# A block-sparse attention and expert kernel on one core: 24 expert tiles in straight code and a jump table for the rest, instead of 31 tiles in straight code

## The chip, the cores and the metric

The kernel runs on one core of one Trainium2 chip. The metric is the device time of one execution in microseconds; lower is better. The time of the kernel before is the median of three executions without a profile. The trace is of one further execution, taken by the hardware profiler.

The engines are named as the profile names them: PE is TensorE (PEld its weight loads), DVE is VectorE, ACT is ScalarE, POOL is GpSimd and SP is SyncE. A trailing q (PEldq, POOLq) marks records of an engine's instruction stream: branches, register loads, semaphore steps.

## The reference

Two parts follow one another. The first is attention over 4 x 8 heads of 768 tokens with a block mask; its result is laid out as x, 3072 tokens of 512 numbers. The second sends each token to one of eight experts:

```python
logits = x @ w_gate                      # (3072, 512) @ (512, 8)
expert_idx = np.argmax(logits, axis=1)
gate_w = probs[np.arange(N), expert_idx]
for e in range(E):                       # rows lo:hi of x_sorted belong to expert e
    h = np.maximum(x_sorted[lo:hi] @ w1[e], 0.0)   # w1[e]: 512 x 1024
    y_sorted[lo:hi] = h @ w2[e]                    # w2[e]: 1024 x 512
return gate_w[:, None] * y_sorted[inv_perm]
```

The inputs are random with a fixed seed, so how many tokens each expert receives is fixed by the reference.

## The kernel before

**Attention** (to about 430 us of the trace). Rows of x, with the gate weight behind them, are written to a scratch tensor x_d in memory, and the logits stay on the chip. Line 371 loads a flag, bad, into a register of each engine, and line 372 skips a slower version of the attention where the flag is zero, as it is here: `again = nc.values_load(bad[0:1, 0:1], min_val=0, max_val=1)`, `with tc.If(again > 0):`.

**Routing** (430 to 479 us, lines 386 to 499). VectorE works out which expert each token goes to, nt_e, how many tiles of 128 tokens each expert needs, and upto, its running sum over the experts. The tokens of an expert start at a new tile. At most NT + E - 1 = 24 + 7 = 31 = NC tiles can result. xe holds the expert of each tile; tiles behind the last used one get expert 7. g_idx holds the row that each place of a tile gathers (row 0 where there is none), s_idx the row that it is scattered to (out of bounds, and so dropped, where there is none).

**Experts** (479 us to the end, lines 502 to 578). For each of the NC = 31 tiles: gather(i) (line 512) fetches 128 rows of x_d by an indirect DMA issued on GpSimd; fetch(i) (lines 519 and 521) loads the tile's expert number into a register of SP, which then issues the load of that expert's w1, 2 MB; turn_x(i) (lines 526, 528) turns the rows by four transposes on PE and a copy on VectorE to xT; layer1(i) (line 538) is 64 instructions of matmul, whose first half of results goes through a relu on VectorE (line 543) and whose second half through one on ScalarE (line 545) into hT; layer2(i) loads the expert number into a register of PE (line 548) and multiplies hT with that expert's w2, which lies in SBUF (line 551, 16 instructions); VectorE scales the result by the gate weight into zo (line 556) and GpSimd issues the indirect DMA that scatters it to the output (line 557). Buffers: xg four, w1, xT, hT, zo two each.

**Order.** The program order is gather and fetch two tiles ahead, then turn_x and layer 1 one tile ahead, then layer 2 of the tile. A scheduler works out each engine's own order from that, by readiness and priority, within one stretch of straight code; nothing is moved into or out of a conditional block. Engines run their own streams and meet at semaphores.

Of the kernel before, what the change touches and what calls it, by code (L numbers as in the profile page):

```python
# [8 lines left out]
F32 = mybir.dt.float32  # L9
BF16 = mybir.dt.bfloat16  # L10
I32 = mybir.dt.int32
AX = mybir.AxisListType.X
AF = mybir.ActivationFunctionType
ALU = mybir.AluOpType
# [4 lines left out]
def kernel(  # L19
# [11 lines left out]
    nc = tc.nc  # L31
# [9 lines left out]
    E = moe_w_gate.shape[1]  # L41
# [3 lines left out]
    NT = N // P  # L45
    NC = NT + E - 1
# [6 lines left out]
    const = ctx.enter_context(tc.tile_pool(name="const", bufs=1))  # L53
# [332 lines left out]
    g_idx = const.tile([P, NC], I32, name="g_idx")  # L386
    s_idx = const.tile([P, NC], I32, name="s_idx")
    xe = const.tile([1, NC], I32, name="xe")

    rt = ExitStack()  # L390
    sm = rt.enter_context(tc.tile_pool(name="sm", bufs=1))
# [55 lines left out]
    nc.vector.reduce_sum(nt_e[:], og[:], axis=AX)  # L447
    upto = sm.tile([P, E], F32, name="upto")
    nc.vector.tensor_tensor_scan(upto[:], nt_e[:], zero_e[:], 0.0, op0=ALU.add, op1=ALU.add)

    xk = sm.tile([1, NC, E], F32, name="xk")
    nc.vector.tensor_tensor(  # L452
# [55 lines left out]
    st = [{} for _ in range(NC)]  # L508

    def gather(i):  # L510
        xg = st[i]["xg"] = xp.tile([P, XW], F32, name="xg", bufs=4)
        nc.gpsimd.indirect_dma_start(  # L512
            out=xg[:], out_offset=None, in_=x_d[:, :],
            in_offset=bass.IndirectOffsetOnAxis(ap=g_idx[:, i : i + 1], axis=0),
        )

    def fetch(i):

        e = nc.sync.value_load(xe[0:1, i : i + 1], min_val=0, max_val=E - 1)
        w1 = st[i]["w1"] = wp.tile([P, DB, F], F32, name="w1")  # L520
        nc.sync.dma_start(w1[:], w1v[:, bass.ds(e, 1)].rearrange("p e c f -> p (e c) f"))

    def turn_x(i):
        tp = ps_m.tile([P, DB, P], F32, name="tpg", tag="m")
        for c in range(DB):
            nc.tensor.transpose(tp[:, c, :], st[i]["xg"][:, c * P : (c + 1) * P], ident[:])  # L526
        st[i]["xT"] = xp.tile([P, DB, P], F32, name="xgT")
        nc.vector.tensor_copy(st[i]["xT"][:], tp[:])  # L528

    def layer1(i):  # L530

        hT = st[i]["hT"] = xp.tile([P, FB, P], F32, name="hT")
        for g in range(2):
            hp = ps_h.tile([P, FB // 2, P], F32, name="hp")
            for m in range(FB // 2):
                fb = g * (FB // 2) + m
                for c in range(DB):
                    nc.tensor.matmul(  # L538
                        hp[:, m, :], lhsT=st[i]["w1"][:, c, fb * P : (fb + 1) * P], rhs=st[i]["xT"][:, c, :],
                        start=(c == 0), stop=(c == DB - 1),  # L540
                    )
            if g == 0:
                nc.vector.tensor_relu(hT[:, : FB // 2, :], hp[:])  # L543
            else:
                nc.scalar.activation(hT[:, FB // 2 :, :], hp[:], AF.Relu)  # L545

    def layer2(i):
        e = nc.tensor.value_load(xe[0:1, i : i + 1], min_val=0, max_val=E - 1)
        zp = ps_z.tile([P, DM], F32, name="zp")
        for fb in range(FB):  # L550
            nc.tensor.matmul(  # L551
                zp[:], lhsT=st[i]["hT"][:, fb, :], rhs=w2_all[:, fb, bass.ds(e, 1), :].rearrange("p e d -> p (e d)"),
                start=(fb == 0), stop=(fb == FB - 1),
            )
        zo = xp.tile([P, DM], F32, name="zo")
        nc.vector.tensor_scalar(zo[:], zp[:], scalar1=st[i]["xg"][:, DM : DM + 1], scalar2=None, op0=ALU.mult)  # L556
        ins = nc.gpsimd.indirect_dma_start(  # L557
            out=out[:, :], out_offset=bass.IndirectOffsetOnAxis(ap=s_idx[:, i : i + 1], axis=0),
            in_=zo[:], in_offset=None, bounds_check=N - 1, oob_is_err=False,
        )  # L560
        ins = getattr(ins, "ins", ins)
        tc.declare_no_dep(ins, group="rows_out", reason="disjoint rows")
        tc.add_to_no_dep_group("rows_out", ins)
        st[i].clear()

    for i in range(2):
        fetch(i)
        gather(i)
    turn_x(0)
    layer1(0)  # L570
    for i in range(NC):
        if i + 2 < NC:
            gather(i + 2)
            fetch(i + 2)
        if i + 1 < NC:
            turn_x(i + 1)
            layer1(i + 1)
        layer2(i)


# [28 lines left out]
```

## Time and profile before

| | us |
|---|---|
| median of three executions (lowest, highest) | 933.06 (931.87, 934.28) |
| the profiled execution | 937.63 |
| its span, first to last instruction | 935.9 |
| PE busy (share of the span) | 881.2 (94%) |
| PE weight loads busy | 562.5 (60%) |
| VectorE, ScalarE, GpSimd busy | 303.1, 206.4, 78.0 |

The page gives busy time by engine, 40 slices of the span, the DMA queues, the chain of work that ended last and the costliest groups of instructions. A matmul's end in the records is modelled, so PE's busy share says when it had work, not how well it was used.

### The profile page before, as it was taken

The page shows a single profiled execution, that of the slowest core. Times are in us where ns is not written, and L with a number is a line of the kernel's source. Part 1 is how long each engine was busy: PE and PEld are TensorE (multiplying, and loading weights), DVE is VectorE, ACT ScalarE, POOL GpSimd, SP SyncE. Part 2 cuts the span into 40 slices and gives each one's busy share as a digit, 9 for nine tenths or more (in the row PEclk, how much of TensorE's full clock was granted, in tenths as well). Part 3 has the DMA queues.
Part 4 walks back from the last instruction along what each step waited for, and adds up shares of the span by engine and source line. Part 5 has one row for each costly group of instructions (what it writes and reads, how often), then busy time and mean ns, then how long its engine had stood idle before and what let it go on. Part 6 is the DMA issues. An engine that isn't in the chain of part 4 may idle for free.

```text
span 935.9 us, 13135 instructions
## 1 busy us (share of the span) xinstructions
PE 881.2 (94%) x5350; PEld 562.5 (60%) x5350; DVE 303.1 (32%) x590; ACT 206.4 (22%) x292; POOL 78.0 (8%) x103
## 2 busy tenths in 40 slices
PE   4999999999999999994479999999999999999997
PEld 2455555555455555542467767677677676776764
DVE  4545555555545555554311111111111111111110
ACT  1534444444544444441000000000000000000000
POOL 5000000000000000001100111101111011010100
PEclk9999999999999999996569999999999999999999
DMA  9992222212222221000146453545545545455320
GB/s 271 374 310 69 68 69 68 60 46 66 69 63 56 69 65 38 18 19 22 58 176 242 178 191 132 213 164 178 197 147 211 183 151 215 157 192 200 138 93 1
DMA packets 96392, 122.57 MB, mean 131 GB/s; under 512 B 56451, under 2 KB 72835, under 8 KB 96324
## 3 DMA queue, kind: packets, MB, share of 16 engines
q1 hardware_dynamic: 86612, 90.28, 29.9%
q0 software_dynamic: 9184, 31.33, 9.7%
q8 instruction: 46, 0.75, 0.3%
q14 instruction: 22, 0.18, 0.1%
q10 hardware_dynamic: 528, 0.02, 0.0%
HBM read 108.93 MB, written 14.52 MB: 132 GB/s over the span
## 4 chain that ended last, share of the span: by engine, by line
issue 46%; POOL 5%; PE 1%; DVE 1%; POOLq 0%; DVEq 0%
POOL xg L512 3%; POOL out_dram L557 1%; PE tok_ps L492 1%; DVE oh_r L487 0%; POOLq L604 0%; DVE oh_c L479 0%; DVE oh_c L483 0%; DVE sl L467 0%; POOLq L512 0%; POOLq L557 0%; DVE pr__10054 L432 0%; PE cps L437 0%; PE cps L438 0%; POOL lt_strict L409 0%; DVE xk L452 0%
## 5 line engine op out<-in xcount | busy, mean ns | idle before, releaser
L538 PEld LDWEIGHTS hp<-xgT,w 128*128 128x128 f32 x1984 | 228.4, 194 | 20.2 <-DVE xgT L528 11.6
L538 PE MATMUL hp<-xgT,w 128*128 128x128 f32 x1984 | 230.0, 277 | 3.5 <-issue 2.5
L551 PE MATMUL zp<-w_all,hT 128*128 x496 | 222.3, 592 | 0.0
L200 ACT ACTIVATE e<-s 128x768 f32<-128x768 f32 x192 | 155.5, 811 | 95.6 <-PE s L198 92.3
L195 PE MATMUL s<-qT,kT 64*128 64x384 f32 x768 | 168.3, 517 | 0.0
L206 DVE TENSOR_TENSOR esum<-esum,e 128x768 f32<-128x768 f32 x128 | 122.7, 958 | 72.6 <-ACT e L200 65.6
L215 PE MATMUL op<-e,v_sb 128*64 128x384 f32 x768 | 144.8, 499 | 0.0
L551 PEld LDWEIGHTS zp<-w_all,hT 128*128 128x128 f32 x496 | 89.8, 190 | 91.3 <-issue 91.3
L545 ACT ACTIVATE hT<-hp 128x512 f32<-128x512 f32 x31 | 18.5, 597 | 468.3 <-PE hp L538 461.8
L556 DVE TENSOR_SCALAR zo<-zp,xg 128x512 f32<-128x512 f32 x31 | 23.3, 751 | 252.8 <-PE zp L551 252.8
L195 PEld LDWEIGHTS s<-qT,kT 64*128 64x128 f32 x768 | 64.5, 189 | 65.1 <-ACT e L200 37.9
L215 PEld LDWEIGHTS op<-e,v_sb 128*64 128x64 f32 x768 | 46.6, 136 | 80.1 <-issue 79.9
L543 DVE TENSOR_SCALAR hT<-hp 128x512 f32<-128x512 f32 x31 | 21.4, 691 | 137.3 <-issue 117.0
L557 POOL DMA_INDIRECT out_dram<-zo,s_idx x31 | 31.5, 1017 | 398.2 <-DVE zo L556 398.2
L198 PE MATMUL s<-pen,oh 64*128 64x384 bf16 x384 | 63.8, 326 | 0.0
L206 DVE TENSOR_TENSOR esum<-e 128x768 f32<-128x768 f32 x32 | 30.6, 958 | 68.6 <-ACT e L200 68.6
L231 PEld LDWEIGHTS xr<-ones,esum 128*128 128x128 f32 x384 | 45.4, 192 | 1.8 <-DVE esum L206 1.2
L231 PE MATMUL xr<-ones,esum 128*128 128x1 f32 x384 | 45.0, 244 | 0.0
L396 POOL IOTA first_w_i<- 128x8 int32 x1 | 0.1, 134 | 423.7 <-SPq L372 423.7
L198 PEld LDWEIGHTS <-oh 64*128 64x128 bf16 x384 | 19.6, 95 | 25.6 <-issue 1.7
L512 POOL DMA_INDIRECT xg<-x_rows,g_idx x31 | 30.3, 976 | 32.0 <-DVE s_idx L498 22.3
L526 PEld LDWEIGHTS tpg<-ident,xg 128*128 128x128 f32 x124 | 16.4, 151 | 25.7 <-issue 25.0
(112 smaller groups left out, 328.0 us busy)
## 6 DMA issues: line engine op xcount, KB each, us to landing
w<-in_moe_w_dram SPq DMA_DIRECT2D x31, 2048.0 KB, 7.8
w_all<-in_moe_w_dram POOLq DMA_DIRECT2D x8, 2048.0 KB, 31.0
k_sb<-in_k_dram SPq DMA_DIRECT2D x32, 192.0 KB, 3.7
q_sb<-in_q_dram SPq DMA_DIRECT2D x32, 192.0 KB, 3.2
v_sb<-in_v_dram SPq DMA_DIRECT2D x16, 384.0 KB, 3.1
x_rows<-xb SPq DMA_DIRECT2D x16, 384.0 KB, 3.7
xg<-x_rows,g_idx POOLq DMA_INDIRECT x31, 3.4
out_dram<-zo,s_idx POOLq DMA_INDIRECT x31, 2.8
```

Of the source, the lines that this page charges most:

```text
L195: nc.tensor.matmul(s[:, hh, :CW], lhsT=kT[r, c * P : (c + 1) * P], rhs=qT[r, cols], start=True, stop=False)
L198: nc.tensor.matmul(s[:, hh, :CW], lhsT=oh[r, c, :], rhs=pen[r, cols], start=False, stop=True)
L200: nc.scalar.activation(e[:], s[:, :, :CW], AF.Exp, scale=scale)
L206: nc.vector.tensor_add(t[:], es[(n, half, 0)][:] if c == 1 else t[:], e[:])
L215: nc.tensor.matmul(op[hh * D : (hh + 1) * D, :], lhsT=v_sb[:, hh, c, :], rhs=e[:, hh, :], start=(c == 0), stop=(c == NCH - 1),)
L231: nc.tensor.matmul(xr[:, HC * M + 2 * m + hh : HC * M + 2 * m + hh + 1], lhsT=esum[:, hh, m * P : (m + 1) * P], rhs=ones[:], start=True, s ...
L512: nc.gpsimd.indirect_dma_start(out=xg[:], out_offset=None, in_=x_d[:, :], in_offset=bass.IndirectOffsetOnAxis(ap=g_idx[:, i : i + 1], axis=0),
L538: nc.tensor.matmul(hp[:, m, :], lhsT=st[i]["w1"][:, c, fb * P : (fb + 1) * P], rhs=st[i]["xT"][:, c, :], start=(c == 0), stop=(c == DB - 1),)
L543: nc.vector.tensor_relu(hT[:, : FB // 2, :], hp[:])
L551: nc.tensor.matmul(zp[:], lhsT=st[i]["hT"][:, fb, :], rhs=w2_all[:, fb, bass.ds(e, 1), :].rearrange("p e d -> p (e d)"), start=(fb == 0), ...
L556: nc.vector.tensor_scalar(zo[:], zp[:], scalar1=st[i]["xg"][:, DM : DM + 1], scalar2=None, op0=ALU.mult)
L557: ins = nc.gpsimd.indirect_dma_start(out=out[:, :], out_offset=bass.IndirectOffsetOnAxis(ap=s_idx[:, i : i + 1], axis=0), in_=zo[:], in_of ...
```

## The change

Routing stays as it is, but two small operations on VectorE are added: they take the last entry of upto, the number of tiles that carry tokens, subtract NT = 24, and keep the result between 0 and 7 as an integer, more. The expert stage runs tiles 0 to 23 in straight code as before, except that gather, fetch and turn_x of tile 24 are issued there too, and layer 1 of tile 24 is not. Then every engine loads more into a register and jumps into one of eight arms. The arm with k tiles holds straight code for tiles 24 to 24 + k - 1 and ends with a jump to a common end. Within an arm the order is gather and fetch of the next tile, layer 1 of this one, turn_x of the next, layer 2 of this one. The tiles and buffers are the same ones; the line that forgot a tile's buffers after its scatter is gone, because several arms name the same buffers.

```diff
--- before.py
+++ after.py
@@ -386,6 +386,7 @@
     g_idx = const.tile([P, NC], I32, name="g_idx")
     s_idx = const.tile([P, NC], I32, name="s_idx")
     xe = const.tile([1, NC], I32, name="xe")
+    more = const.tile([1, 1], I32, name="more")
 
     rt = ExitStack()
     sm = rt.enter_context(tc.tile_pool(name="sm", bufs=1))
@@ -447,6 +448,12 @@
     nc.vector.reduce_sum(nt_e[:], og[:], axis=AX)
     upto = sm.tile([P, E], F32, name="upto")
     nc.vector.tensor_tensor_scan(upto[:], nt_e[:], zero_e[:], 0.0, op0=ALU.add, op1=ALU.add)
+
+    more_f = sm.tile([1, 1], F32, name="more_f")
+    nc.vector.tensor_scalar(
+        more_f[:], upto[0:1, E - 1 : E], scalar1=float(-NT), scalar2=0.0, op0=ALU.add, op1=ALU.max,
+    )
+    nc.vector.tensor_scalar_min(more[:], more_f[:], float(NC - NT))
 
     xk = sm.tile([1, NC, E], F32, name="xk")
     nc.vector.tensor_tensor(
@@ -561,21 +568,32 @@
         ins = getattr(ins, "ins", ins)
         tc.declare_no_dep(ins, group="rows_out", reason="disjoint rows")
         tc.add_to_no_dep_group("rows_out", ins)
-        st[i].clear()
+
 
     for i in range(2):
         fetch(i)
         gather(i)
     turn_x(0)
     layer1(0)
-    for i in range(NC):
-        if i + 2 < NC:
+    for i in range(NT):
+        if i + 2 <= NT:
             gather(i + 2)
             fetch(i + 2)
-        if i + 1 < NC:
+        if i + 1 <= NT:
             turn_x(i + 1)
+        if i + 1 < NT:
             layer1(i + 1)
         layer2(i)
+
+    for extra in tc.Switch(nc.values_load(more[0:1, 0:1], min_val=0, max_val=NC - NT), NC - NT + 1):
+        for i in range(NT, NT + extra):
+            if i + 1 < NT + extra:
+                gather(i + 1)
+                fetch(i + 1)
+            layer1(i)
+            if i + 1 < NT + extra:
+                turn_x(i + 1)
+            layer2(i)
 
 
 # ---- launch: one core; inputs and outputs as the reference has them ----
```

## Rows read from the trace of the kernel before

**Rows 1.** The page's slices: busy tenths of PE.

```profile
PE   4999999999999999994479999999999999999997
```

**Rows 2.** Table by stage: us, then busy us (instructions) of each engine.

```profile
core 0: us, PE busy (x) PEld busy (x) DVE busy (x) ACT busy (x) POOL busy (x), PEclk, DMA share, GB/s
503.00:821.00 318.00, 318.00 (x1847) 232.50 (x1845) 44.38 (x66) 13.13 (x22) 43.90 (x44) 1.00 0.51 179
821.00:931.00 110.00, 108.99 (x600) 75.73 (x598) 14.29 (x22) 4.18 (x7) 12.98 (x13) 1.00 0.35 125
```

**Rows 3.** Timeline of two middle tiles: start us, duration us, engine, line, operation.

```profile
719.10 0.75 DVE L556 TENSOR_SCALAR zo<-zp,xg 128x512 f32<-128x512 f32 x1 [7.98 <-PE zp L551]
733.56 0.75 DVE L556 TENSOR_SCALAR zo<-zp,xg 128x512 f32<-128x512 f32 x1 [7.61 <-PE zp L551]
```

**Rows 4.** Timeline of the last tiles, same columns.

```profile
909.45 0.75 DVE L556 TENSOR_SCALAR zo<-zp,xg 128x512 f32<-128x512 f32 x1 [8.83 <-PE zp L551]
910.86 7.22 PEld L538 LDWEIGHTS hp<-xgT,w 128*128 128x128 f32 x64 [0.97 <-DVE xgT L528]
914.79 0.69 DVE L543 TENSOR_SCALAR hT<-hp 128x512 f32<-128x512 f32 x1 [3.99 <-issue]
918.11 13.04 PE L551 MATMUL zp<-w_all,hT 128*128 x30
924.32 0.75 DVE L556 TENSOR_SCALAR zo<-zp,xg 128x512 f32<-128x512 f32 x1 [8.84 <-PE zp L551]
931.18 0.75 DVE L556 TENSOR_SCALAR zo<-zp,xg 128x512 f32<-128x512 f32 x1 [6.12 <-PE zp L551]
```

**Rows 5.** DMA after 896 us: queue, packets, MB; then issues and landing.

```profile
q0 software_dynamic: 320, 0.07, 0.8%
out_dram<-zo,s_idx POOLq DMA_INDIRECT x4, 2.1
```

**Rows 6.** Timeline of VectorE in the routing stage.

```profile
445.19 0.17 DVE L457 TENSOR_SCALAR xe_f<-xe_f 1x31 f32<-1x31 f32 x1
```

**Rows 7.** Lines L371 and L372: durations in ns (min/median/max), first and last start.

```profile
L371 PEldq TENSOR_LOAD <-bad x1: 494/494/494, 433.4 to 433.4; - x1
L372 SPq EVENT_SEMAPHORE  x8: 17/17/17, 437.7 to 438.2; - x8
L372 POOLq COMPARE_BRANCH  x1: 45/45/45, 433.9 to 433.9; - x1
L372 PEldq COMPARE_BRANCH  x1: 3967/3967/3967, 434.0 to 434.0; - x1
L372 SPq COMPARE_BRANCH  x1: 50/50/50, 435.2 to 435.2; - x1
```

**Rows 8.** Line L396, GpSimd's first instructions after that branch.

```profile
L396 POOLq EVENT_SEMAPHORE  x7: 42/43/43, 437.8 to 438.4; - x7
```

**Rows 9.** Lines L512 (gathers) and L521 (w1 loads): us from issue to landing.

```profile
DMA to landing us min/median/max: 3.2/3.4/5.3
...
DMA to landing us min/median/max: 7.4/7.8/15.4
```

**Rows 10.** Lines L548 and L604: instruction streams of PE and GpSimd.

```profile
L548 PEldq TENSOR_LOAD <-xe x9: 297/300/307, 800.3 to 917.7; - x9
...
L604 POOLq DRAIN  x3: 51/109/2942, 932.0 to 935.6; - x3
L604 PEldq DRAIN  x2: 13/3964/7915, 923.3 to 935.4; - x2
```

**Rows 11.** Table by stage around PE's idle time, columns as in rows 2.

```profile
431.00:432.00 1.00, 0.00 (x0) 0.00 (x0) 0.93 (x6) 0.14 (x1) 0.00 (x0) 0.50 0.15 45
...
482.00:486.00 4.00, 4.00 (x26) 4.00 (x25) 0.40 (x1) 0.00 (x0) 0.00 (x0) 0.64 0.02 4
```

**Rows 12.** Timeline of the first layer 1.

```profile
478.91 17.38 PE L538 MATMUL hp<-xgT,w 128*128 128x128 f32 x128 [2.49 <-issue]
485.61 0.69 DVE L543 TENSOR_SCALAR hT<-hp 128x512 f32<-128x512 f32 x1 [11.73 <-PE hp L538]
```

## The prediction

> **What bounds the kernel now.** I read the page's time slices first: the TensorE (PE) row is at nine tenths almost throughout, with one dip in the middle [rows 1]. Then the table by stage [rows 2]: from 503 to 821 us PE is busy 318.00 of 318.00 us, from 821 to 931 us 108.99 of 110. These are the expert tiles, and no other engine is busy there for more than a seventh of the time, so a microsecond of PE work taken out of this stage is a microsecond of the kernel. One tile is 64 matmuls of layer 1 (910.86 to 918.11, 7.25 us [rows 4]), 16 of layer 2 and four transposes. In the timeline [rows 3] the zo of successive tiles starts at 719.10 and 733.56, a period of 14.46 us. Near the end [rows 4] the period is 14.87 (909.45, 924.32): layer 1 there waits for the copy of xT (0.97 us of idle weight loads at 910.86). After the last zo at 931.18 the span ends at 935.9, 4.7 us later.
>
> How many of the 31 tiles carry tokens follows from the reference: its router sends 431, 32, 256, 32, 256, 160, 593 and 1312 tokens to the eight experts, which is 4+1+2+1+2+2+5+11 = 28 tiles of 128. The trace agrees: after 896 us the scatters of tiles 27 to 30 (four issues) move 0.07 MB [rows 5]; the 32 rows left over in tile 27 (1312 - 10 x 128), 2 KB each, are 0.066 MB, so tiles 28 to 30 write nothing. The count less 24 is 4: the arm with four tiles runs.
>
> **The change, part by part.** I call E the end of layer 2 of tile 23, the last PE work ahead of the jump.
>
> Removed: three tiles of PE work, at the end of the stage where one costs 14.87: 3 x 14.87 = 44.6 us (43.4 at the earlier period).
>
> Moved: in the arm the order is layer 1 of tile i, transposes of i+1, layer 2 of i. Layer 2 no longer has another tile's layer 1 between it and its own. Its first matmuls read the half of hT that VectorE writes when layer 1 is half done; the half that ScalarE writes after layer 1, in a relu of the size of VectorE's (0.69 us [rows 4]), is needed only eight matmuls later, 8 x 13.04/30 = 3.5 us after layer 2 began [rows 4]. So this order costs nothing, and xT of i+1 has a whole layer 2 for its copy: the 0.41 us per tile (14.87 - 14.46) lost at the end now should not come in the arm's three later tiles, at most -1.2 us. I take -0.6. The w1 of tile 25 waits only for layer 1 of tile 23, some 14 us before E, and lands 7.8 us later [rows 9]: hidden. Later fetches have the same distance. If that cover were gone, 7.8 us a tile would show.
>
> Added on VectorE: two one-element operations in the routing chain, which runs without a gap to the token matmuls. Nearest row: L457, an operation of the same kind on 31 elements, 0.17 us [rows 6]: twice that, +0.35 (0 to 0.4).
>
> Added on every engine: a register load and an indirect jump. The kernel has one such place, the load of `bad` and the skipped block at L371 and L372 [rows 7]. There PE's load took 0.49 us and its branch 3.97. On SP and GpSimd the branch itself is 50 and 45 ns, but the next instruction comes late: SP's from 435.2 to 437.7, GpSimd's from 433.9 to 437.8 [rows 7, 8]. So a jump costs 2.5 to 4.0 us of an engine's instruction stream. [...]
>
> What of that reaches PE's array? PE's instruction stream runs ahead of it: it arrived at the closing DRAIN at 923.3, while the array worked until 918.11 + 13.04 = 931.15 [rows 4, 10]. The lead is 7.8 us. The jump needs 0.49 + 3.97 and some 0.3 for register arithmetic, 4.8 in all; the loads of expert numbers in the arm, 0.30 each [rows 10] and as much again for arithmetic, are another 2.4 if all four come first. 7.2 is less than 7.8: I take 0. The lower end is 0, because the jump does no work; the upper end is the full 4.8 with an idle array, plus the clock. [...] The first half of that layer took 485.61 - 478.91 = 6.70 us to its relu [rows 12] against 914.79 - 910.86 = 3.93 [rows 4], 2.8 us more. Upper end 7.6.
>
> Queued behind the jump elsewhere: ScalarE and SP pass it long before E, their work for tile 23 being done or queued. VectorE passes after zo of 23, about E + 4, and its next work is due with half of layer 1, about E + 3.9: slack in any case, since layer 2 comes later. GpSimd matters: the gather of tile 25 now stands behind the scatter of tile 23 and the jump. The scatter leaves its sequencer 0.8 us after zo begins (931.18 and 932.0 [rows 4, 10]), so at about E + 0.9; load 0.5, jump 3.9, handing over 0.2, landing 3.4 [rows 7 to 9]: the rows are there at E + 8.9. The transposes of tile 25 are due after layer 1 of tile 24, E + 7.25 (910.86 to 918.11 [rows 4]). PE waits 1.6: I take +1.5. Lower end 0 (transposes placed within layer 2, as they are today); upper end a landing of 5.3, as the slowest gather, and a lost clock: 3.5 + 2.8 = 6.3. Gathers of 26 and 27 need no such wait, as each has a full tile.
>
> Added at the end: each engine jumps from the arm to the common end, and semaphores that the shorter arm didn't raise are raised (SP's eight at L372, 437.7 to 438.2). GpSimd is last, after the scatter of tile 27. The jump there is unhidden in part, because the scatter needs 2.1 us to land [rows 5]. Bounds 0 (all behind the landing) to 5 (4.0 of jump and 0.5 of semaphores behind it, and a little); I take the fastest jump, SP's: +2.5.
>
> Sum: -44.6 - 0.6 + 0.35 + 0 + 1.5 + 2.5 = -40.85 us. The profiled execution took 937.63 us with a span of 935.9; the runs without a profile have a median of 933.06. The change is a difference within the span, so 933.06 - 40.85 = 892.2 us.
>
> **The rivals.** First: the jump is not hidden, PE's array is empty when it is taken, or the arm's first instructions arrive late. For it: PE's branch record is itself 3.97 us long, unlike the others', which may mean that PE does more there [rows 7]; that the array was idle at that time, so the rows can't show overlap. Against it: the lead of 7.8. Price 7.6, less the 1.5 for the gather which then has time: 898.3 us. [...]
>
> Second: code comes late inside the arm as well. Four tiles are some 4 x (2 x 64 + 2 x 4 + 2 x 16 + 20) = 750 PE instructions; if two further pieces of code have to be waited for at 4.0 each, it is +8: 900.2 us. Against it: the static tiles run the same number of instructions with PE never idle [rows 2].
>
> Third, on the other side: the idle time at the jump drops the clock to 0.50 and it stays there in the arm. A tile then takes twice 14.46; four are 57.8 more: 892.2 + 57.8 + 3.3 = 953 us. It decides the sign from (40.85 - 3.3)/14.46 = 2.6 tiles at the low clock. Against it: the clock came back within the first layer 1, from 482 to 486 us [rows 11].
>
> Fourth: the change doesn't do what it says; the count comes out as 7 and all 31 tiles run. Then nothing is removed and 0.35 + 1.5 + 2.5 are added: 937.4 us. The bytes of the scatters speak against it [rows 5].
>
> **How the numbers follow.** Forecast 0.66, first rival 0.20, second 0.10, third 0.02, fourth 0.02. Low: all credits and no costs, -44.6 - 1.2 + 0.2 = -45.6, so 887. High: the first rival with the end term at its bound and a late gather as well, 898.3 + 2.5 + 2 = 903, which takes in most of the second. A difference under 0.3% (2.8 us) can't be told from no change here. Faster 0.96: the first three cases; slower 0.03: the last two; same 0.01.
>
> **What would show it.** In the timeline after: PE has no idle time longer than 1 us at the jump, then up to 1.6 before the transposes of tile 25; the zo of the last tile starts near 888 us and 28 of them are there; L538 has 28 x 64 matmuls; the span ends 7 us after the last zo. A granted clock under 1.00 after 503 us, or PE idle for 4 us between tiles 23 and 24, would make the first rival right. 31 zo would make the fourth right. An end term over 5 us or idle time between layer 1 and layer 2 in each tile of the arm would make the sum wrong.

## The result and the profile after

The changed kernel takes 896.71 us (median of four executions, 893.64 to 902.72) against 933.67 for the kernel before on the same chip: a ratio of 0.961, 95% interval 0.956 to 0.967. The gain is 37.0 us; the sum had 40.85. The profiled execution took 896.5 us with a span of 894.8.

The page's first lines and PE's slices (busy tenths), which answer to rows 1:

```profile
span 894.8 us, 12581 instructions
PE   3999999999999999999058999999999999999887
```

The dip of the routing is where it was. New are the two slices at eight tenths just ahead of the last one. The table by stage (columns as in rows 2), cut at the last zo of straight code and the last zo of all:

```profile
500.00:823.30 323.30, 323.30 (x1852) 234.33 (x1852) 44.27 (x66) 13.13 (x22) 43.92 (x44) 1.00 0.51 177
823.30:888.30 65.00, 59.90 (x332) 43.25 (x330) 7.87 (x12) 2.39 (x4) 6.89 (x7) 0.97 0.27 95
888.30:894.80 6.50, 0.00 (x0) 0.00 (x0) 0.71 (x1) 0.00 (x0) 0.98 (x1) 0.86 0.05 15
```

Straight code keeps PE busy throughout, as in rows 2. In the arm PE is idle for 5.1 of 65.0 us and the clock is 0.97. PE's timeline across the jump and through the arm shows where (layer 1 is L545 now, the transposes L533, layer 2 L558; the brackets give the idle time before and what ended it):

```profile
816.22 7.03 PE L558 MATMUL zp<-w_all,hT 128*128 x16
823.09 7.31 PE L545 MATMUL hp<-xgT,w 128*128 128x128 f32 x64
832.66 0.66 PE L533 MATMUL tpg<-ident,xg 128*128 128x128 f32 x4 [2.26 <-DMA xg<-x_rows,g_idx]
833.52 7.13 PE L558 MATMUL zp<-w_all,hT 128*128 x16 [0.20 <-issue]
...
855.67 7.38 PE L545 MATMUL hp<-xgT,w 128*128 128x128 f32 x64 [0.24 <-DMA w<-in_moe_w_dram]
...
863.00 7.03 PE L558 MATMUL zp<-w_all,hT 128*128 x16
872.34 9.01 PE L545 MATMUL hp<-xgT,w 128*128 128x128 f32 x64 [2.31 <-DMA w<-in_moe_w_dram]
```

Layer 1 of tile 24, the first work behind the jump, begins while layer 2 of tile 23 ends: the jump costs the array nothing. Then come three waits: 2.26 us for the gather of tile 25, 0.24 and 2.31 us for the w1 of tiles 26 and 27. The layer 1 behind the last takes 9.01 us instead of 7.31.

The jump itself, by the lines of the load and of the switch (columns as in rows 7):

```profile
L588 PEldq TENSOR_LOAD <-more x1: 307/307/307, 816.0 to 816.0; - x1
L622 PEldq COMPARE_BRANCH  x1: 3634/3634/3634, 816.7 to 816.7; - x1
L588 PEldq BRANCH_PREFETCH_HINT  x1: 55/55/55, 820.4 to 820.4; - x1
...
L622 POOLq COMPARE_BRANCH  x1: 43/43/43, 824.7 to 824.7; - x1
L588 POOLq BRANCH_PREFETCH_HINT  x1: 64/64/64, 827.5 to 827.5; - x1
L622 POOLq INC_SWDGE_SEM  x2: 807/834/860, 827.6 to 829.1; - x2
```

PE's stream loads the count at 816.0, when the array has layer 2 of tile 23 still ahead of it (816.22 to 823.25), and is in the arm at 820.4, when the array still has 2.85 us of that layer to do. GpSimd branches at 824.7 and runs its first instruction in the arm at 827.5. Then it spends 0.8 us on a semaphore step (INC_SWDGE_SEM); the trace before has this instruction only at its start, at 0.2 us, 31 ns long. The trace of the kernel below that runs seven tiles in the arm has none behind its jump: in the traces here the step comes with the arm of four tiles only.

Two lines of GpSimd and one of VectorE: the gather of tile 25, the last zo and the last scatter.

```profile
829.34 0.99 POOL L519 DMA_INDIRECT xg<-x_rows,g_idx  x1 [4.04 <-DMA xg<-x_rows,g_idx]
...
888.26 0.75 DVE L563 TENSOR_SCALAR zo<-zp,xg 128x512 f32<-128x512 f32 x1 [9.68 <-PE zp L558]
...
890.17 0.98 POOL L564 DMA_INDIRECT out_dram<-zo,s_idx  x1 [18.09 <-issue]
```

The w1 loads that the arm issues for tiles 26 and 27, SP's line L528 from 825 us on:

```profile
L528 SPq DMA_DIRECT2D w<-in_moe_w_dram x2: 372/372/373, 847.8 to 863.1; - x2
...
DMA to landing us min/median/max: 7.7/8.4/9.1
```

The load of tile 26 is issued at 847.8, when layer 1 of tile 25 ends (840.48 + 7.31). The sum had it at the end of layer 1 of tile 24, 830.4. From 847.8 to 855.5 it has only a transpose and a layer 2 to hide behind.

### The profile page after: what moved, and what is told of

Its sections match the earlier page's. It is cut to its first block, busy times and chain, and to the rows that moved or that the text cites. A ratio compares the mean times of both kernels' runs of the same rounds, so it can differ in the third digit from the quotient of the medians.

```text
span 894.8 us, 12581 instructions
## 1 busy us (share of the span) xinstructions
PE 835.8 (93%) x5098; PEld 531.3 (59%) x5098; DVE 297.6 (33%) x583; ACT 204.5 (23%) x289; POOL 71.5 (8%) x97
## 4 chain that ended last, share of the span: by engine, by line
issue 38%; DMA 5%; POOL 4%; another core or an unknown queue 2%; PE 1%; DVE 1%; POOLq 0%; DVEq 0%
DMA out_dram<-zo,s_idx 5%; POOL xg L519 3%; PE tok_ps L499 1%; POOL out_dram L564 1%; DVE oh_r L494 0%; DVE oh_c L486 0%; DVE oh_c L490 0%; DVE sl L474 0%; PE cps L438 0%; DVE pr__10055 L433 0%; POOLq L519 0%; POOLq L564 0%; PE cps L439 0%; POOL lt_strict L410 0%
## 5 line engine op out<-in xcount | busy, mean ns | idle before, releaser
L545 PEld LDWEIGHTS hp<-xgT,w 128*128 128x128 f32 x1792 | 208.1, 195 | 17.9 <-issue 13.1
L545 PE MATMUL hp<-xgT,w 128*128 128x128 f32 x1792 | 208.6, 279 | 5.0 <-DMA w<-in_moe_w_dram 2.6
L558 PE MATMUL zp<-w_all,hT 128*128 x448 | 200.3, 593 | 0.2 <-issue 0.2
L558 PEld LDWEIGHTS zp<-w_all,hT 128*128 128x128 f32 x448 | 81.5, 191 | 84.5 <-issue 84.5
L552 ACT ACTIVATE hT<-hp 128x512 f32<-128x512 f32 x28 | 16.7, 597 | 437.1 <-PE hp L545 430.6
L563 DVE TENSOR_SCALAR zo<-zp,xg 128x512 f32<-128x512 f32 x28 | 21.0, 750 | 219.8 <-PE zp L558 219.8
L550 DVE TENSOR_SCALAR hT<-hp 128x512 f32<-128x512 f32 x28 | 19.4, 691 | 125.3 <-issue 88.7
L564 POOL DMA_INDIRECT out_dram<-zo,s_idx x28 | 28.4, 1015 | 363.3 <-DVE zo L563 345.2
L236 PE MATMUL xr<-mix,oT 128*128 128x144 f32 x192 | 31.4, 300 | 0.0
L533 PE MATMUL tpg<-ident,xg 128*128 128x128 f32 x112 | 19.0, 296 | 12.3 <-DMA xg<-x_rows,g_idx 12.3
```

Of the source, the lines that this page charges most:

```text
L236: nc.tensor.matmul(xr[:, m * M : (m + 1) * M], lhsT=oT[:, m * P : (m + 1) * P], rhs=mix[:, pr, :], start=True, stop=True)
L545: nc.tensor.matmul(hp[:, m, :], lhsT=st[i]["w1"][:, c, fb * P : (fb + 1) * P], rhs=st[i]["xT"][:, c, :], start=(c == 0), stop=(c == DB - 1),)
L558: nc.tensor.matmul(zp[:], lhsT=st[i]["hT"][:, fb, :], rhs=w2_all[:, fb, bass.ds(e, 1), :].rearrange("p e d -> p (e d)"), start=(fb == 0), ...
L564: ins = nc.gpsimd.indirect_dma_start(out=out[:, :], out_offset=bass.IndirectOffsetOnAxis(ap=s_idx[:, i : i + 1], axis=0), in_=zo[:], in_of ...
```

## The experiments

Times are medians in us; the ratio is to the kernel before measured beside it, with its 95% interval. Theory A is that the jump is hidden by PE's lead and that the arm loses time to two things: GpSimd's late gather, and a w1 buffer that tile 24 keeps. Its rivals are named with each run.

**28 tiles in straight code.** No jump; what does the arm cost as a whole?

```diff
-    for i in range(NC):
-        if i + 2 < NC:
+    NU = 28
+    for i in range(NU):
+        if i + 2 < NU:
...
-        if i + 1 < NC:
+        if i + 1 < NU:
```

> The kernel before with its loop over tiles cut to 28, in straight code: no count, no jump, and tiles 28 to 30, which carry no token, are left out. It prices the jump and its arms as a whole. Theory A (the arm costs the gather's wait, two waits for w1 with a slow stretch after one of them, and a later end: 2.3 + 4.2 + 1.8 us in the trace after, less about 1 us from a better order): 933.7 - 44.6 = 889.1 us, some 7.6 below the changed kernel's 896.7. Rival B (the 3.9 us by which the measured median lies above the sum are variation between executions, the jump is free): 893 to 895, within 4 us of the changed kernel.

Measured: 892.21, ratio 0.956 (0.952 to 0.959). That lies between the two theories' numbers and its interval overlaps the changed kernel's, so the time alone decides nothing. It lies above A's 889 for two reasons that the record shows. The kernel before took 934.48 beside it and not 933.7, and with 28 tiles in straight code the last scatter is late too. Straight code also ends with the slow period, but A's 889.1 had that in it (14.87 a tile).

```profile
862.43 0.75 DVE L556 TENSOR_SCALAR zo<-zp,xg 128x512 f32<-128x512 f32 x1 [8.83 <-PE zp L551]
877.29 0.75 DVE L556 TENSOR_SCALAR zo<-zp,xg 128x512 f32<-128x512 f32 x1 [8.84 <-PE zp L551]
884.16 0.75 DVE L556 TENSOR_SCALAR zo<-zp,xg 128x512 f32<-128x512 f32 x1 [6.12 <-PE zp L551]
...
886.08 0.98 POOL L557 DMA_INDIRECT out_dram<-zo,s_idx  x1 [6.76 <-issue]
```

The period is 14.86, and the last scatter starts 1.92 us after its zo, where the kernel before has 1.03 (932.21 - 931.18 in its timeline). So 0.9 us of the changed kernel's later end belongs to the 28 tiles and not to the jump. A's sum then becomes 934.48 - 44.6 + 0.9 = 890.8; the four executions lie between 891.34 and 896.70, and the last 1.4 us stay unexplained.

**Gather ahead of the jump.**

```diff
+        gather(i + 2)
         if i + 2 <= NT:
-            gather(i + 2)
             fetch(i + 2)
...
-                gather(i + 1)
+                if i > NT:
+                    gather(i + 1)
```

> The changed kernel with the gather of tile 25 issued ahead of the jump. Theory A: the wait of 2.26 us ahead of the transposes of tile 25 was for that gather alone, which stood behind GpSimd's jump: it is gone, 896.7 - 2.3 = 894.4 us, and the waits for w1 of tiles 26 and 27 remain. Rival B: PE is held there by its own jump, and the gather only ended last: 896 to 897 us, PE idle at the same place with another releaser.

Measured: 891.49, ratio 0.954 (0.951 to 0.957). PE's timeline, the transposes of tile 25 and layer 1 of tile 27:

```profile
830.44 0.60 PE L533 MATMUL tpg<-ident,xg 128*128 128x128 f32 x4
...
868.77 7.38 PE L545 MATMUL hp<-xgT,w 128*128 128x128 f32 x64 [1.50 <-DMA w<-in_moe_w_dram]
```

The wait is gone, so it was the gather's alone. The gain is larger than A's 2.3, because the wait for tile 27's w1 is shorter too (1.50 against 2.31) and the layer 1 behind it runs at full speed (7.38). Why that load landed sooner isn't shown.

**Two w1 buffers in turn.**

```diff
+    w1_two = [wp.tile([P, DB, F], F32, name=f"w1_{j}", bufs=1) for j in range(2)]
...
-        w1 = st[i]["w1"] = wp.tile([P, DB, F], F32, name="w1")
+        w1 = st[i]["w1"] = w1_two[i % 2]
```

> The changed kernel with two w1 buffers named once and used in turn, in place of two buffers taken from a rotating pool. Theory A (tile 24's w1 is taken ahead of the switch and kept until behind it, so the arms have one w1 buffer, and the load of tile 26 waits for layer 1 of tile 25): the load of tile 26 is issued when layer 1 of tile 24 ends, some 17 us earlier, PE's waits of 0.24 and 2.31 us for w1 and the slow layer 1 behind the second (9.01 against 7.31 us) go: 896.7 - 4.2 = 892.5 us. Rival B (the load of tile 26 is late because SP reaches it late, or because its transfer is slowed by gathers): the issue stays at the end of layer 1 of tile 25, 896.7 us.

Measured: 893.54, ratio 0.955 (0.953 to 0.958). SP's loads from 825 us on, and PE's timeline:

```profile
L529 SPq DMA_DIRECT2D w<-in_moe_w_dram x2: 372/372/373, 832.4 to 849.8; - x2
...
834.63 0.66 PE L534 MATMUL tpg<-ident,xg 128*128 128x128 f32 x4 [2.27 <-DMA xg<-x_rows,g_idx]
...
871.32 7.31 PE L546 MATMUL hp<-xgT,w 128*128 128x128 f32 x64
```

The load of tile 26 is issued at 832.4, when layer 1 of tile 24 ends (825.05 + 7.31), and no wait for w1 is left. The wait for the gather stands as before, 2.27. Nothing but the buffers was changed, so the late loads come from the way they were taken. In the changed kernel tile 24's w1 was taken ahead of the switch, and its buffer was not given back inside the arm: the loads of tiles 26 and 27 (847.8 and 863.1) are each issued as the layer 1 one tile ahead ends, as with a single buffer.

**Both.** The two edits above in one kernel.

> The changed kernel with both: the gather of tile 25 ahead of the jump, and two w1 buffers in turn. Theory A: both waits go, 896.7 - 2.3 - 4.2 = 890.2 us, PE without idle time from tile 0 to tile 27 across the jump, and what is left above the 28 tiles in straight code is the end, about 1.8 us. Rival B (something else in the arm is next in line, such as the copy of xT or GpSimd's instructions): 892 to 895 us with a new wait.

Measured: 889.60, ratio 0.951 (0.948 to 0.953): the lowest median of this study, ahead of both given kernels. PE's branch, and its transposes of tile 25 and layer 1 of tile 27, which have no idle time before them:

```profile
L624 PEldq COMPARE_BRANCH  x1: 5425/5425/5425, 818.4 to 818.4; - x1
...
831.97 0.60 PE L534 MATMUL tpg<-ident,xg 128*128 128x128 f32 x4
...
868.17 7.31 PE L546 MATMUL hp<-xgT,w 128*128 128x128 f32 x64
```

PE's branch took 5.42 us here and 3.63 in the changed kernel, for the same jump. It is still hidden, but with 1.1 us to spare: the branch ends at 823.87, layer 2 of tile 23 at 824.99. Over the nine traces with the jump PE's branch took 3.35 to 5.42 us.

**The count comes late.** This takes PE's lead away from the jump: the count is written only behind the zo of tile 23, by an operation that adds zero times an element of that zo to it.

```diff
-    nc.vector.tensor_scalar_min(more[:], more_f[:], float(NC - NT))
+    nc.vector.tensor_scalar_min(more_c[:], more_f[:], float(NC - NT))
...
+    nc.vector.scalar_tensor_tensor(
+        more[:], in0=st[NT - 1]["zo"][0:1, 0:1], scalar=0.0, in1=more_c[:], op0=ALU.mult, op1=ALU.add,
+    )
     for extra in tc.Switch(
```

> The changed kernel with the count made late: one VectorE operation behind zo of tile 23 adds zero times an element of it to the count, and the load ahead of the jump waits for that, so PE's queue is empty when it jumps. Theory A (in the changed kernel PE's jump of 3.63 us is hidden by the 7 us by which its instruction stream runs ahead of its array): now some 1.0 + 0.3 + 0.2 + 3.6 + 0.4 = 5.5 us of PE idle time stand between tiles 23 and 24, and layer 1 of tile 24 runs partly at a granted clock under 1.00, up to 2.8 us more; the 2.3 us of waiting for the gather go, since it now has time: 896.7 + 5.5 + 2.8 - 2.3 = 902.7 us, or 900 if the clock holds. Rival B (the jump costs the array the same wherever the count comes from): at most 1 us more, 897.7 us.

Measured: 901.38, ratio 0.964 (0.962 to 0.966). PE's branch, layer 1 of tile 24 and the stages around it:

```profile
L626 PEldq COMPARE_BRANCH  x1: 3548/3548/3548, 828.0 to 828.0; - x1
...
831.93 8.92 PE L546 MATMUL hp<-xgT,w 128*128 128x128 f32 x64 [5.74 <-issue]
...
830.00:832.00 2.00, 0.07 (x1) 0.10 (x1) 0.00 (x0) 0.00 (x0) 0.00 (x0) 0.50 0.13 29
832.00:834.00 2.00, 2.00 (x10) 2.00 (x11) 0.00 (x0) 0.00 (x0) 0.49 (x1) 0.50 0.20 45
```

The branch takes about as long as in the changed kernel, 3.55 us, but now PE's array stands still for 5.74 us, the granted clock is 0.50 when layer 1 begins, and that layer takes 8.92 instead of 7.31. In this trace tile 24's zo starts 21.96 us after tile 23's (848.19 and 826.23), in the changed kernel 17.39 (840.68 and 823.29). A is right within its two numbers, 900 and 902.7, and the wait for the gather of tile 25 is gone, as it had said. The jump is the same instruction in both kernels; what it cost the array went with the work that PE had queued: nothing in the changed kernel, 5.74 us of idle time here. What the branch spends its 3.55 us on, no run here shows.

**All 31 tiles, seven of them in the arm.** The count is forced to 7.

```diff
-        more_f[:], upto[0:1, E - 1 : E], scalar1=float(-NT), scalar2=0.0, op0=ALU.add, op1=ALU.max,
+        more_f[:], upto[0:1, E - 1 : E], scalar1=float(-NT), scalar2=float(NC - NT), op0=ALU.add, op1=ALU.max,
```

> The changed kernel with the count forced to 7: all 31 tiles run, 24 in straight code and 7 in the arm, the three empty ones as well. It sets the arm against straight code with the same tiles. Theory A (the arm has one w1 buffer, so each tile from 26 on waits for its load): five tiles wait, 0.5 to 4 us each, some 10 in all, + 2.3 for the gather + 0.9 at the end - 2.9 for the order: 934 + 10 = 944 us, slower than the kernel before. Rival B (the waits at tiles 26 and 27 come from something that happens once, at the end or at the jump): 934 + 2.3 + 4.2 + 0.9 - 2.9 = 938 us.

Measured: 938.43, ratio 1.003 (1.001 to 1.005). That is B's number. The trace is A's: five loads, each issued as a layer 1 ends, and a wait at each tile from 26 on (tiles 26, 27 and 30 shown; 28 and 29 wait 0.57 and 0.58 in the same timeline).

```profile
L528 SPq DMA_DIRECT2D w<-in_moe_w_dram x5: 373/373/373, 848.9 to 910.1; - x5
...
856.88 7.38 PE L545 MATMUL hp<-xgT,w 128*128 128x128 f32 x64 [0.42 <-DMA w<-in_moe_w_dram]
...
872.20 7.38 PE L545 MATMUL hp<-xgT,w 128*128 128x128 f32 x64 [0.52 <-DMA w<-in_moe_w_dram]
...
918.35 7.38 PE L545 MATMUL hp<-xgT,w 128*128 128x128 f32 x64 [1.38 <-DMA w<-in_moe_w_dram]
```

So A named the mechanism and priced it too high: 0.4 to 0.6 us a tile. The last tile pays more, 1.38: no transposes of a next tile (0.44 us) stand between layer 2 and its layer 1, and its load took 8.08 us where tile 29's took 7.72.

A also had 2.3 us for the gather of tile 25. Its wait is shorter here:

```profile
833.73 0.66 PE L533 MATMUL tpg<-ident,xg 128*128 128x128 f32 x4 [1.34 <-DMA xg<-x_rows,g_idx]
```

GpSimd has no INC_SWDGE_SEM in this arm, and the gather starts at 830.22, 3.92 us after the scatter ahead of it (826.30); in the changed kernel it is 5.02 (829.34 - 824.32). So about a microsecond of the changed kernel's wait goes with that step.

**All 31 tiles, with both mends.** The count forced to 7 as above, and the two edits of the gather and the buffers.

> The count forced to 7, all 31 tiles, with the gather of tile 25 ahead of the jump and two w1 buffers used in turn. Theory A (then the jump and the arm cost PE nothing, and only the end is later): 934 - 2.9 + 0.9 = 932 us, not to be told from the kernel before. Rival B (arm code has a price of its own for each tile, for instance fetched code or GpSimd's extra instructions): 936 us or more, PE idle time between the tiles of the arm.

Measured: 932.10, ratio 0.996 (0.995 to 0.998): a little faster than 31 tiles in straight code. Two successive zo in the arm, as most there follow one another:

```profile
897.18 0.75 DVE L564 TENSOR_SCALAR zo<-zp,xg 128x512 f32<-128x512 f32 x1 [6.18 <-PE zp L559]
911.63 0.75 DVE L564 TENSOR_SCALAR zo<-zp,xg 128x512 f32<-128x512 f32 x1 [6.18 <-PE zp L559]
```

14.45 us, where the kernel before has 14.87 at its end [rows 4]. B, a price of arm code for each tile, falls. One interval in the arm is longer, 14.97 (867.76 to 882.73). The gather of tile 28, which started late (last section), landed only at 874.71, when its transposes were due. PE's stream waited there, loaded the expert number of tile 27 only behind them (874.76), and layer 2 began 0.4 us late.

**63 DMAs on GpSimd instead of 64.** The kernel with both mends; the w2 load of the last expert goes to SP.

```diff
-        nc.gpsimd.dma_start(w2_all[:, :, e, :], moe_w2[e].rearrange("(a p) d -> p a d", p=P))
+        eng = nc.sync if e == E - 1 else nc.gpsimd
+        eng.dma_start(w2_all[:, :, e, :], moe_w2[e].rearrange("(a p) d -> p a d", p=P))
```

> The kernel with both mends (gather of tile 25 ahead of the jump, two w1 buffers in turn), and the w2 load of the last expert issued on SP instead of GpSimd, so that GpSimd issues 63 DMAs instead of 64. Theory A (GpSimd's 64th DMA starts some 0.9 us late whatever it is; with 28 tiles it is the last scatter, and with 31 tiles it lies in the middle, where six traces have it): the last scatter starts 1.03 us after its zo instead of 1.91, and the end term is shorter by 0.9 us: about 888.7 us. Rival B (the last scatter is late because of the code behind it, the jump to the end or the last raising of semaphores): it stays at 1.91, 889.6 us.

Measured: 906.23, ratio 0.969 (0.968 to 0.970). The start of the last scatter is as A has it, 1.02 us after its zo:

```profile
893.31 0.75 DVE L565 TENSOR_SCALAR zo<-zp,xg 128x512 f32<-128x512 f32 x1 [9.68 <-PE zp L560]
...
894.33 0.98 POOL L566 DMA_INDIRECT out_dram<-zo,s_idx  x1 [13.03 <-DVE zo L565]
...
L625 POOLq DRAIN  x3: 51/109/5276, 898.5 to 904.4; - x3
```

The time didn't follow. The new load on SP delayed the attention's loads behind it (the next one of k is issued at 16.36 and the one after that at 26.78, against 16.00 and 16.59 with both mends; layer 1 of tile 0 starts at 487.52 in this trace against 476.86 with both mends), and a DRAIN of GpSimd of 5.28 us now ends the kernel, 0.99 us long in the kernel with both mends. So the late start goes with the count of 64 and not with the code behind it, but whether the end can be made shorter by it stays open.

**The changed kernel again**, beside the last one.

> The changed kernel, unaltered, beside the kernel with both mends on one chip. Theory A (the w1 loads of tiles 26 and 27 are exposed, and how far depends on each load's time; 2.31 us and a slow layer 1 behind it were a long case): the waits for w1 differ from execution to execution, the trace has the load of tile 26 issued at the end of layer 1 of tile 25 again, and the median lies at 893 to 897 us, 4 to 8 above the mended kernel. Rival B (the waits are always those of the first trace): 896 to 897 us, with the same two waits within 0.2 us.

Measured: 897.34, ratio 0.959 (0.958 to 0.961). PE's timeline, tile 25's transposes and tile 27's layer 1:

```profile
833.92 0.66 PE L533 MATMUL tpg<-ident,xg 128*128 128x128 f32 x4 [2.21 <-DMA xg<-x_rows,g_idx]
...
873.48 9.01 PE L545 MATMUL hp<-xgT,w 128*128 128x128 f32 x64 [2.26 <-DMA w<-in_moe_w_dram]
```

The same waits within 0.1 us: B. The 2.3 us at tile 27 is no long case: both traces of this kernel have it. Why the load takes 9.1 us there and 7.7 to 8.1 in the kernel with seven tiles in the arm isn't settled.

## Why the prediction was right, and where it was short

The measured gain is 37.0 us where the sum had 40.85, and the time 896.7 where it had 892.2, within the range of 887 to 903. Step by step:

**Three tiles of PE work, -44.6.** Right: 28 zo are in the trace, and L545 has 28 x 64 = 1792 matmuls on the page. Without the jump the price shows alone: from the first zo to the last, 28 tiles in straight code take 383.33 us (500.83 to 884.16), 31 take 427.93 (503.25 to 931.18), which is 44.6 more. The count was 4, so the fourth rival falls.

**The arm's order, -0.6.** Right in sign, too small. Two kernels with 28 tiles and no wait for a DMA show it alone: from the first zo to the last, straight code takes 383.33 us and the kernel with both mends 381.69 (500.70 to 882.39), 1.64 less. That is four times 0.41: straight code runs four intervals at 14.86 or 14.87, the arm none. The prediction had counted three tiles at most, -1.2.

**VectorE, +0.35.** In its range, nearer the lower end. The two operations, in VectorE's timeline of the changed kernel:

```profile
440.64 0.14 DVE L453 TENSOR_SCALAR more_f<-upto 1x1 f32<-1x1 f32 x1
...
441.04 0.13 DVE L456 TENSOR_SCALAR more<-more_f 1x1 int32<-1x1 f32 x1
```

They lie between operations of the chain that overlap in the records. From the start of upto to the token matmuls the chain takes 7.37 us (440.44 to 447.81) where the kernel before takes 7.29 (444.10 to 451.39): +0.08.

**PE's jump, 0.** Right, and for the reason given. The stream reached the jump at 816.0, 7.3 us before the last zo of straight code (823.29), against a lead of 7.8 read at the end of the kernel before; load and branch took 4.4. The expert numbers were loaded later, tile by tile, and not ahead of layer 1. The first rival falls, and the run with the late count shows what it would have cost. The 2.8 us of lost clock in its price of 7.6 were read from layer 1 of tile 0 in the trace before [rows 12]; layer 1 behind the late count lost 1.6 (8.92 against 7.31). The second falls too: in the arm of the kernel with both mends PE has no idle time before a layer 1. A granted clock under 1.00 after 503 us, named as a sign for the first rival, did occur, from 872 us on, but behind a wait for w1 some 50 us after the jump. The margin was partly luck: the branch took 3.63 us here, and the 5.42 us of the kernel with both mends left 1.1 us.

**The gather of tile 25, +1.5.** The mechanism was right, the size short: 2.26. GpSimd was in the arm at 827.5, 4.3 us after E (823.25), a microsecond sooner than reckoned. But the gather was issued at 829.34, 6.1 us after E and not 5.5, behind the semaphore step of 0.8 us, which the trace before could not show. Landing took 3.3. With seven tiles in the arm, where there is no such step, the wait is 1.34, close to the forecast. The prediction had put semaphores that a short arm doesn't raise at the end alone; on GpSimd one stood ahead of the first gather.

**The later loads of w1, "later fetches have the same distance".** This is the step that failed. It read the buffers as a rotation of two that goes on through the arm. Tile 24's w1 belongs to code outside the switch, so its buffer came back only behind it, and the loads of tiles 26 and 27 had one buffer between them. Each was issued a whole tile late; the buffers named once and used in turn bring both loads forward and end the waits. The cost is 0.24 + 2.31 + 1.70 = 4.25 us, the last part from the lower clock behind the second wait. The prediction named the price of lost cover as 7.8 us a tile; in fact layer 2 still covers most of the 7.7 to 9.1 us.

**The end, +2.5.** 6.5 us from the last zo to the end of the span instead of 4.7, so +1.8. Half of it, 0.9, is the late start of the last scatter (890.17 - 888.26 = 1.91), which 28 tiles in straight code have as well. What the jump adds is about 0.9 (6.5 against 5.6 in straight code), less than the fastest jump seen before.

**The terms as measured.** The intervals between zo give the waits with all that hangs on them: 17.39, 14.45, 14.94 and 18.19 us from tile 23 to 27 in the changed kernel, 14.45, 14.45, 14.45 and 14.02 with both mends. So the gather cost 2.9 and the loads of w1 4.7. Then -44.6 - 1.6 + 0.1 + 2.9 + 4.7 + 1.8 = -36.7, and the medians give -37.0. The sum's -40.85 was short by 4.7 for w1 and 1.4 for the gather; the order, VectorE and the end came out 2.0 us better than forecast, so the time came as near as it did in part because errors cancelled.

That the two profiled executions differ by 41.1 us, almost the sum, is in part luck: the first layer 1 starts at 478.91 [rows 12] in the one and at 475.14 in the other, behind code that is the same but for the two operations. The profiled execution of before was 4 us above its kernel's median. The medians are the fairer measure.

**The third rival**, the clock that stays low in the arm, falls, but its first half did happen, at another place than the jump. The table by stage of the changed kernel, around the two long waits:

```profile
830.30:833.50 3.20, 0.75 (x5) 0.42 (x4) 0.15 (x1) 0.60 (x1) 1.94 (x3) 1.00 0.59 164
...
872.00:874.00 2.00, 1.66 (x9) 1.69 (x10) 0.00 (x0) 0.00 (x0) 0.08 (x1) 0.64 0.34 131
874.00:878.00 4.00, 4.00 (x29) 4.00 (x29) 0.11 (x1) 0.00 (x0) 0.00 (x0) 0.75 0.00 0
```

After the wait of 2.31 us the granted clock was 0.64 and then 0.75 on average; it was 1.00 from 878 to 882 us, and so back before the layer ended (881.35), at a price of 1.70 us.

## What to carry to other kernels

Skipping work by a jump table was free here on the engine that bounds the kernel, because that engine had enough queued work when it came to the jump and the index was computed long before: a lead of 7 us against 4.1 to 6.1 for load and branch. With the index late it cost 5.74 us of idle time and a slow restart (layer 1 in 8.92 us instead of 7.31). What must be looked at instead are the other engines' instructions that now stand behind the jump (the gather of tile 25 cost 2.26 us of waiting), and every buffer that crosses it: the w1 buffer taken ahead of the switch and read inside it wasn't given back there, so a rotation of two became one, and the load of tile 26 was issued as layer 1 of tile 25 ended, at 847.8 us; with two named buffers it was issued at 832.4, as layer 1 of tile 24 ended. On GpSimd the arm of four tiles also had semaphore steps (five of 0.81 to 0.86 us) that the arm of seven has not, one of them ahead of its first gather. Name such buffers once and use them in turn, and issue the first transfer of the arm ahead of the jump: the two together gave 7.1 us here (896.7 to 889.6, ratio 0.961 to 0.951).

## What the runs showed that was not expected

**One late DMA in 64.** GpSimd issues eight loads of w2, and then gathers and scatters. The 64th of all starts late in each of the ten traces that have one. In the kernels with 28 tiles that is the last scatter, 1.91 or 1.92 us after its zo instead of 1.03. With 31 tiles it lies earlier. In the kernel before it is a gather, 1.91 us behind the scatter ahead of it, where others have 1.32 (822.62 - 821.30); there it was hidden:

```profile
865.89 1.02 POOL L557 DMA_INDIRECT out_dram<-zo,s_idx  x1 [12.57 <-DVE zo L556]
867.80 0.97 POOL L512 DMA_INDIRECT xg<-x_rows,g_idx  x1 [0.89 <-issue]
```

With seven tiles in the arm it is the scatter of tile 26, at 873.19, 1.91 us after its zo at 871.28. With seven tiles and both mends it is the gather of tile 28, at 870.76, 1.97 us behind its scatter (868.79); this is what made one interval there 14.97 instead of 14.45. What GpSimd does then was not found out.

**Waits of one length, and not one outcome.** Of the changed kernel's two long waits, 2.26 and 2.31 us, only the second was followed by a lower granted clock. Ahead of the first PE ran layer 1, 64 matmuls in 7.3 us; ahead of the second layer 2, 16 in 7.0 us. That difference alone doesn't decide it. In the kernel with the late count PE waits 2.22 us behind the same layer 2, and layer 1 runs at full speed, with a granted clock of 1.00 throughout:

```profile
879.75 7.38 PE L546 MATMUL hp<-xgT,w 128*128 128x128 f32 x64 [2.22 <-DMA w<-in_moe_w_dram]
```

The changed kernel's second trace has 2.26 us there and a layer 1 of 9.01. The wait of 1.50 us in the kernel with the early gather, also behind a layer 2, left layer 1 at full speed (7.38). The study doesn't tell what decides.
